# A fused attention and feed-forward block: four weight transfers by group, and two collections of the attention output in two pieces

## The chip, the core and the metric

The kernel runs on one core of one Trainium2 chip. The metric is the device time of one execution in microseconds (us), lower is better. The kernel before has a median of 215.92 us over three runs (215.3 to 215.97).

The core's engines run beside one another and wait for each other by semaphores: TensorE (PE, with its weight loads as PEld) multiplies matrices, VectorE (DVE), ScalarE (ACT) and GpSimd (POOL) work on tiles, and SyncE (SP) issues transfers. Sixteen DMA engines carry the transfers; SP and ACT each have a queue of them (q1 is SP's in the profile, q10 is ACT's).

## The reference

S = 2048 tokens, D = 448 columns, H = 16 heads of 28, F = 1792, an attention window of W = 256; all arrays are bfloat16.

```python
xn = _layernorm(x)
qkv = (xn @ wqkv).reshape(B, S, 3, H, Dh).transpose(2, 0, 3, 1, 4)
q, k, v = qkv[0], qkv[1], qkv[2]
scores = einsum("bhqd,bhkd->bhqk", q, k) * (Dh ** -0.5)
mask = (i - j >= 0) & (i - j < W)
p = softmax(where(mask, scores, -1e9))
o = einsum("bhqk,bhkd->bhqd", p, v)
attention = o.transpose(0, 2, 1, 3).reshape(B, S, D) @ wo
ffn = (gelu(xn @ w_gate) * (xn @ w_up)) @ w_down
return x + attention + ffn
```

## The kernel before

The tokens are cut into 16 tiles of 128 (t) and four blocks of 512 (qb, 0 to 3). The normalised input stands transposed in `xnT` (columns in four chunks of up to 128 partitions), and once more in `xsw` with the two halves of each chunk exchanged, so that two matmuls with 64 rows each can run on the two halves of the array. The feed-forward part reads both: a pair of matmuls per chunk, one from `xnT`, one from `xsw` (L459).

The 16 heads are four groups of four (g). The weights of q and k for all heads arrive in `wraw`, q in columns 0 to 447 and k in columns 448 to 895. Each group is then copied into `wqp` (q) or `wkp` (k), where a head has 32 columns instead of 28 (`pads`, L711 to L716). `proj` (L189 to L232) multiplies them with `xnT` into the PSUM tiles `pq` and `pk`, `qk_halves` (L197) adds the last 64 columns, and `qk_copies` (L244, L245) moves the results to `qT` and `kT`.

The order of the work is written out by hand; an engine, and the SP queue, run their instructions in the order in which the code names them. The order at the start is this. SP issues x tiles 0, 2 and 3, weights of v, the last rows of the weights (L92, L94), x tiles 4 to 7 (L95), and then at L97 the columns of groups two to four, once for q, once for k. ACT issues x tile 1 and group one of q and k (L89). Behind L97, SP issues the first part of the up weights `wu` (L82), `w3k` (L130), the exchange of `xsw` for block 0 (`swap`, L440), x tiles 8 to 11 (L745), the transposition of tile 4 (L176), the exchanged v weights `wvs` (L776) and three more transpositions. VectorE copies, behind `qk_copies` of group one (L762 to L769): group two of q, a tile of v, group two of k, groups three and four of q, groups three and four of k; then it normalises tile 4. TensorE meanwhile projects group two, computes scores (L657) as soon as the score buffer is free, and after the projections of group four begins with the up projection (`gen_up`, tile `ue`), whose first chunk reads `xsw`. There is one score buffer during attention, which the exponential on ScalarE (L661) empties.

Every transfer counts its landing on one of eight semaphores in turn (SP's and ACT's transfers together); an issue waits until the transfer eight places before it, which used the same semaphore, has landed.

Block by block, attention and the feed-forward part of one block are woven together with the output part (`gen_down`, L393) of the block before. The head dimension 28 leaves four of 32 rows unused, so heads 14 and 15 are spread over these rows. For the output this means: the fourth group's tile of `oN`, rows 64 to 123, is collected into a buffer `o3` in device memory (`o_collect`, L351, three transfers of 28, 16 and 12 rows of 512 columns) and delivered from there to the four spare rows of each 32 (`o_deliver`, L356, four transfers). `o_finish` then clears or copies rows of `oN` on GpSimd (L362 to L365), and TensorE reads them in the output part of the next block (L410 for blocks 0 and 1, the terms `os` for blocks 2 and 3). `hook` (L850) calls these after a step of the gate, `o_collect` from SP for blocks 1 to 3 and from ACT for block 0.

```python
        for t0, n, p0 in ((0, 7, 64), (7, 4, 96), (11, 3, 112)):
            queue.dma_start(out=o3[t0:t0 + n]..., in_=oNs[qb][p0:p0 + 4 * n, 3, :])
```

The later weights come in `ahead3`: the rest of the gate weights `wg` (groups of three and four column pairs), of `wu`, the output weights `wo` (L798, L799) and `wd`.

Of the kernel before, what the change touches and what calls it, by code (L numbers as in the profile page):

```python
# [16 lines left out]
S, D, H, Dh, F = 2048, 448, 16, 28, 1792  # L17
# [10 lines left out]
def kernel(  # L28
# [11 lines left out]
    nc = tc.nc  # L40
# [25 lines left out]
    wraw = blk.tile([P, 4, 2 * D], bf16, name="wraw", tag="hT")  # L66
# [5 lines left out]
    def rows(w, c0, n):  # L72
        return w[c0 * P:(c0 + n) * P, :].rearrange("(c p) n -> p c n", p=P)

    def load_ffn(dst, w, pairs):

        wv64 = w.rearrange("(c p) (h n) -> p c h n", p=64, h=2)
        ns = slice(pairs.start * P, pairs.stop * P)  # L80
        for hi in range(2):
            nc.sync.dma_start(out=dst[64 * hi:64 * hi + 64, :, ns], in_=wv64[:, :, hi, ns])  # L82

    wqk = rows(A_wqkv, 0, 3)[:, :, 0:2 * D]
# [8 lines left out]
    for a in range(2):  # L93
        nc.sync.dma_start(out=wv[64 * a:64 * a + 64, 3, :], in_=A_wqkv[384:448, 2 * D:3 * D])  # L94
    nc.sync.dma_start(out=x_sb[:, 4:8, :], in_=xv[:, 4:8, :])  # L95
    for c in (0, D):
        nc.sync.dma_start(out=wraw[:, 0:3, c + 4 * Dh:c + D], in_=wqk[:, :, c + 4 * Dh:c + D])  # L97
    load_ffn(wu, B_w_up, slice(0, 5))

    ident = const.tile([P, P], bf16, name="ident")  # L100
# [246 lines left out]

    def o_collect(qb, queue):

        for t0, n, p0 in ((0, 7, 64), (7, 4, 96), (11, 3, 112)):  # L350
            queue.dma_start(out=o3[t0:t0 + n].rearrange("t i n -> (t i) n"), in_=oNs[qb][p0:p0 + 4 * n, 3, :])  # L351

    def o_deliver(qb):
# [450 lines left out]
    for qb in range(NB):  # L804
# [45 lines left out]
        def hook(f):  # L850
            after(f)
            if qb in (1, 2) and f == 0:
                collect(qb + 1)
            if f == (8, 2, 2, 6)[qb]:
                o_collect(qb, nc.sync if qb else nc.scalar)
            if f == (12, 4, 4, 6)[qb]:
                o_deliver(qb)
                o_finish(qb)
            if qb == 0 and f == 6:
                nc.gpsimd.tensor_copy(out=wo[64:128, 3, :], in_=wo[0:64, 3, :])  # L860
            if qb in (1, 2) and f == 10:
                deliver(qb + 1)
            t = ({0: 8, 4: 9, 8: 10, 10: 11} if qb == 0 else {4: 12, 6: 13, 8: 14, 10: 15} if qb == 1 else {}).get(f)
            if t is not None:
                norm(t)
                dma_transp(t)
# [160 lines left out]
```

## Time and profile before

| | us |
|---|---|
| median of three runs | 215.92 |
| lowest and highest | 215.3, 215.97 |
| the profiled execution's own time | 215.69 |
| its span in the profile | 213.9 |
| TensorE busy in it | 208.2 |
| VectorE, ScalarE, GpSimd busy | 161.3, 130.4, 49.4 |

The granted TensorE clock is 1.0 throughout. The span runs from the first to the last instruction of the core; 1.8 us of the execution's time lie around it. A row of the timeline gives start, length, engine, line, operation, tile written and tiles read, how many instructions are merged in it, and in brackets the idle time before it with what ended it. A row with SPq or ACTq is the issue of a transfer, not the transfer. Matmuls overlap one another: one of 512 columns is shown with 0.38 us, but the next starts 0.216 us later.

### The profile page before, as it was taken

The page shows a single profiled execution, that of the slowest core. Times are in us where ns is not written, and L with a number is a line of the kernel's source. Part 1 is how long each engine was busy: PE and PEld are TensorE (multiplying, and loading weights), DVE is VectorE, ACT ScalarE, POOL GpSimd, SP SyncE. Part 2 cuts the span into 40 slices and gives each one's busy share as a digit, 9 for nine tenths or more (in the row PEclk, how much of TensorE's full clock was granted, in tenths as well). Part 3 has the DMA queues.
Part 4 walks back from the last instruction along what each step waited for, and adds up shares of the span by engine and source line. Part 5 has one row for each costly group of instructions (what it writes and reads, how often), then busy time and mean ns, then how long its engine had stood idle before and what let it go on. Part 6 is the DMA issues. An engine that isn't in the chain of part 4 may idle for free.

```text
span 213.9 us, 6417 instructions
## 1 busy us (share of the span) xinstructions
PE 208.2 (97%) x2718; PEld 100.6 (47%) x2722; DVE 161.3 (75%) x357; ACT 130.4 (61%) x121; POOL 49.4 (23%) x85
## 2 busy tenths in 40 slices
PE   7999999999999999999999999999999999999993
PEld 2433444444454545444445435444444444544892
DVE  7799998999767995796536998494449699569531
ACT  4699578566677986423777896532678577456000
POOL 5286758451000211041000202022000021106001
PEclk9999999999999999999999999999999999999999
DMA  6999989979420101003521000101000000000011
GB/s 177 274 223 213 106 199 236 216 220 181 110 56 26 36 0 41 9 5 65 74 74 46 25 0 27 22 0 35 12 26 3 21 3 25 21 3 2 26 44 50
DMA packets 23993, 15.67 MB, mean 73 GB/s; under 512 B 9208, under 2 KB 23832, under 8 KB 23960
## 3 DMA queue, kind: packets, MB, share of 16 engines
q1 hardware_dynamic: 22918, 14.87, 31.7%
q8 instruction: 22, 0.36, 0.7%
q10 hardware_dynamic: 1042, 0.34, 0.7%
q14 instruction: 11, 0.09, 0.1%
HBM read 9.26 MB, written 2.41 MB: 55 GB/s over the span
## 4 chain that ended last, share of the span: by engine, by line
PE 92%; DMA 5%; issue 1%; ACTq 0%; DVE 0%; DVEq 0%
PE po L393 26%; PE gt L459 20%; PE u L459 12%; PE ue L459 8%; PE pq L334 7%; PE sc L657 6%; DMA wraw<-in_A_wqkv_dram 5%; PE ov L627 5%; PE pv L320 4%; PE pq L191 2%; PE pk L191 1%; PE pv L191 0%; PE pq L254 0%; PE po L410 0%; PE pv L197 0%
## 5 line engine op out<-in xcount | busy, mean ns | idle before, releaser
L661 ACT ACTIVATE p_sb<-sc 128x2048 bf16<-128x2048 f32 x39 | 73.2, 1878 | 19.7 <-PE sc L657 12.1
L594 POOL TENSOR_TENSOR oN<-oc,l 128x512 bf16<-128x512 f32 x16 | 22.4, 1409 | 121.8 <-DVE l L607 121.8
L499 ACT ACTIVATE p_sb<-gt 128x1024 bf16<-128x1024 f32 x28 | 28.7, 1025 | 33.6 <-PE gt L459 30.7
L393 PE MATMUL po<-wd,hT 128*128 128x448 bf16 (+1 forms) x266 | 46.4, 324 | 0.0
L459 PE MATMUL gt<-xnT,wg 64*128 64x512 bf16 x224 | 45.6, 376 | 0.0
L459 PE MATMUL gt<-xsw,wg 64*128 64x512 bf16 x168 | 40.7, 376 | 0.0
L575 DVE TENSOR_TENSOR p_sb<-p_sb,masks 128x256 bf16<-128x256 bf16 (+1 forms) x90 | 30.3, 391 | 8.9 <-ACT p_sb L661 8.9
L507 DVE TENSOR_TENSOR hT<-p_sb,u 128x512 bf16<-128x512 bf16 x34 | 21.9, 677 | 16.0 <-PE u L459 15.8
L393 PEld LDWEIGHTS <-hT 128*128 128x128 bf16 x266 | 24.6, 98 | 16.2 <-issue 1.2
L459 PEld LDWEIGHTS <-wg 64*128 64x128 bf16 x392 | 18.6, 94 | 23.0 <-issue 1.3
L459 PEld LDWEIGHTS <-wu 64*128 64x128 bf16 x392 | 18.4, 94 | 23.1 <-issue 2.2
L459 PE MATMUL u<-xnT,wu 64*128 64x512 bf16 x136 | 28.1, 376 | 0.0
L459 PE MATMUL u<-xsw,wu 64*128 64x512 bf16 x102 | 24.7, 376 | 0.0
L382 DVE TENSOR_TENSOR res<-po,x_sb 128x448 bf16<-128x448 f32 (+1 forms) x17 | 9.9, 591 | 12.4 <-PE po L393 10.3
L459 PE MATMUL ue<-xnT,wu 64*128 64x512 bf16 x88 | 18.3, 377 | 0.0
L459 PE MATMUL ue<-xsw,wu 64*128 64x512 bf16 x66 | 16.5, 377 | 0.0
L657 PE MATMUL sc<-qT,kT 28*64 28x320 bf16 (+7 forms) x648 | 16.4, 261 | 0.0
L585 POOL TENSOR_SCALAR_AFFINE_SELECT p_sb<-p_sb 128x512 bf16<-128x512 bf16 (+1 forms) x21 | 14.2, 703 | 6.7 <-ACT p_sb L661 6.7
L657 PEld LDWEIGHTS <-kT 28*64 28x64 bf16 (+1 forms) x648 | 7.7, 102 | 13.4 <-issue 12.2
L393 PE MATMUL po<-wo,oN 128*128 128x448 bf16 (+1 forms) x72 | 13.7, 321 | 0.0
L476 DVE CAST hT<-ue 128x512 bf16<-128x512 f32 x20 | 12.8, 680 | 0.8 <-PE ue L459 0.6
L612 DVE TENSOR_TENSOR oc<-oc,ov 128x512 f32<-128x512 f32 x12 | 8.2, 686 | 5.0 <-ACT oc L611 4.9
(108 smaller groups left out, 274.4 us busy)
## 6 DMA issues: line engine op xcount, KB each, us to landing
out_dram<-res SPq DMA_DIRECT2D x15, 112.0 KB
x_sb<-in_A_x_dram SPq DMA_DIRECT2D x3, 448.0 KB
wd<-in_B_w_down_dram SPq DMA_DIRECT2D x3, 448.0 KB
xsw<-xnT SPq DMA_DIRECT2D x6, 192.0 KB
wu<-in_B_w_up_dram SPq DMA_DIRECT2D x2, 560.0 KB
wg<-in_B_w_gate_dram SPq DMA_DIRECT2D x2, 448.0 KB
wg<-in_B_w_gate_dram SPq DMA_DIRECT2D x2, 336.0 KB
wraw<-in_A_wqkv_dram SPq DMA_DIRECT2D x2, 252.0 KB
```

Of the source, the lines that this page charges most:

```text
L334: nc.tensor.matmul(ps, lhsT=w.rearrange("p h d -> p (h d)"), rhs=xchunk(qb, hi, c, qb * QB, QB), start=c == 0, stop=c == 6, tile_position= ...
L393: nc.tensor.matmul(po[:, a:b], lhsT=x[:, k, tt * P:(tt + 1) * P], rhs=wt[:, k, lo + a:lo + b], start=start and n == a == 0, stop=stop and ...
L459: nc.tensor.matmul(ps, lhsT=w[64 * hi:64 * hi + 64, c, p * P:(p + 1) * P], rhs=xchunk(qb, hi, c, qb * QB, QB), start=c == 0, stop=c == 6, ...
L476: copy(out=hTs[qb][:, p + 7 * i, :], in_=us[i])
L499: nc.scalar.activation(out=ges[p][:, :, :], in_=gt[:, :, :], func=ACT.Gelu_apprx_tanh)
L507: nc.vector.tensor_tensor(out=hT[:, p + 7 * i, :], in0=ge[:, i, :], in1=u, op=ALU.mult)
L575: nc.vector.tensor_tensor(out=reg, in0=reg, in1=m, op=ALU.mult)
L585: nc.gpsimd.affine_select(out=reg, in_=reg, pattern=mid + [[1 if diag else -1, min(w, P)]], compare_op=ALU.is_ge, fill=0.0, base=0 if diag ...
L594: nc.gpsimd.tensor_tensor(out=oN[:, g, :], in0=oc[:, :], in1=inv, op=ALU.mult)
L627: nc.tensor.matmul(ov[half or 0][32 * j:32 * j + 32, q0:q0 + nq], lhsT=v_sb[r, kt, 4 * g + j, :], rhs=p_sb[r, j, col:col + nq], start=n == ...
L657: nc.tensor.matmul(ss[k0:k0 + nk, j, col:col + nq], lhsT=kT[r, g, kt * P + k0:kt * P + k0 + nk], rhs=qT[r, g, ring(qb).start + q0:ring(qb) ...
L661: nc.scalar.activation(out=p_sb[:, :, 0:ncol], in_=ss[:, :, 0:ncol], func=ACT.Exp, scale=SCALE)
```

## The change

Two edits. The columns of groups two to four of `wraw`, which came in one transfer of 336 columns for q and one of 336 for k, come in four: group two of q (112 columns), group two of k, groups three and four of q (224 columns), groups three and four of k. `o_collect` issues, for blocks 1 and 2, two transfers of 28 rows each instead of three of 28, 16 and 12; the rows are the same, since the second and third piece lie next to each other on both sides. Blocks 0 and 3 keep three.

```diff
-    for c in (0, D):
-        nc.sync.dma_start(out=wraw[:, 0:3, c + 4 * Dh:c + D], in_=wqk[:, :, c + 4 * Dh:c + D])
+    for lo, up in ((4 * Dh, 8 * Dh), (8 * Dh, D)):
+        for c in (0, D):
+            nc.sync.dma_start(out=wraw[:, 0:3, c + lo:c + up], in_=wqk[:, :, c + lo:c + up])
...
-        for t0, n, p0 in ((0, 7, 64), (7, 4, 96), (11, 3, 112)):
+        for t0, n, p0 in ((0, 7, 64), (7, 7, 96)) if qb in (1, 2) else ((0, 7, 64), (7, 4, 96), (11, 3, 112)):
             queue.dma_start(out=o3[t0:t0 + n].rearrange("t i n -> (t i) n"), in_=oNs[qb][p0:p0 + 4 * n, 3, :])
```

With this, VectorE's copies wait for four different landings: group two of q for the first transfer, group two of k for the second, groups three and four for the third and the fourth. The lines behind the edit are numbered one higher in the changed kernel.

## The prediction

> **What bounds the kernel now.** I read the page's first part, then the chain of waits, then the stretch that the chain names, in the timeline. The chain rows are start, length, what.
>
> ```profile
> span 213.9 us, 6417 instructions
> PE 208.2 (97%) x2718; PEld 100.6 (47%) x2722; DVE 161.3 (75%) x357; ACT 130.4 (61%) x121; POOL 49.4 (23%) x85
> 7.12 5.54 DMA wraw<-in_A_wqkv_dram
> 12.68 0.29 DVE wkp L716
> 13.02 0.82 PE pk L191 x3
> ```
>
> TensorE is busy for 208.2 of 213.9 us. The chain is TensorE from 13.02 on; before that it hangs on one transfer, the k weights of groups two to four (the second one of L97), which are issued at 7.12 and landed at 12.66. A table by stretch says how much later waiting there is (columns: stretch and length, then busy us of PE, PEld, DVE, ACT and POOL, granted clock, DMA share, GB/s).
>
> ```profile
> 8.00:9.00 1.00, 1.00 (x10) 0.49 (x8) 0.55 (x3) 0.85 (x2) 0.00 (x0) 1.00 1.07 339
> 14.00:19.00 5.00, 5.00 (x39) 1.76 (x37) 4.79 (x12) 4.53 (x7) 3.77 (x7) 1.00 1.38 235
> 16.00:18.40 2.40, 2.40 (x19) 0.83 (x18) 2.26 (x6) 2.07 (x5) 1.79 (x4) 1.00 1.12 254
> 23.30:28.00 4.70, 4.70 (x54) 1.92 (x52) 4.56 (x11) 3.19 (x3) 2.63 (x8) 1.00 0.65 143
> 32.00:43.00 11.00, 11.00 (x140) 4.96 (x134) 9.74 (x19) 7.85 (x8) 7.02 (x10) 1.00 1.04 224
> 104.00:154.00 50.00, 49.95 (x725) 23.64 (x724) 33.51 (x73) 31.62 (x27) 5.84 (x5) 1.00 0.13 29
> ```
>
> From 14 us on TensorE has next to no idle time. So nothing behind that point can be gained by a wait that goes away, and whatever TensorE loses near the start it carries to the end. At the same time the DMA engines are full (share 1.0 and more) from 8 to 18.4 us and from 32 to 43 us, so a transfer made slower there pushes all that stand behind it.
>
> **The weights, part one: the wait that goes away.** These are timeline rows, with the idle time before them in brackets.
>
> ```profile
> 11.55 0.27 DVE L716 COPY wqp<-wraw 128x336 bf16<-128x336 bf16 x1
> 11.73 0.61 DVE L227 CAST v_sb<-pv 128x448 bf16<-128x448 f32 x1
> 12.02 0.82 PE L191 MATMUL pq<-xnT,wqp 128*128 128x512 bf16 x2
> 12.19 1.88 ACT L661 ACTIVATE p_sb<-sc 128x2048 bf16<-128x2048 f32 x1 [0.27 <-PE sc L657]
> 12.68 0.28 DVE L716 COPY wkp<-wraw 128x336 bf16<-128x336 bf16 x1 [0.35 <-DMA wraw<-in_A_wqkv_dram]
> 12.88 0.45 DVE L716 COPY wqp<-wraw 128x672 bf16<-128x672 bf16 x1
> 13.25 0.37 DVE L716 COPY wkp<-wraw 128x672 bf16<-128x672 bf16 x1
> 14.28 0.40 PE L657 MATMUL sc<-qT,kT 28*128 28x384 bf16 x8
> 17.81 1.88 ACT L661 ACTIVATE p_sb<-sc 128x2048 bf16<-128x2048 f32 x1
> 19.79 0.40 PE L657 MATMUL sc<-qT,kT 28*128 28x128 bf16 x8
> ```
>
> VectorE stood idle 0.35 us before it could copy group two of k. With the change this copy waits for the second of four transfers, whose last byte is number 168 KB of the stream. The q transfer of before, with 252 KB, had landed by 11.55, since its copy ran then. So the new piece lands by about 11.6 at the latest, the copy runs at 12.33, right behind the cast that starts at 11.73, and pk can follow pq without the gap: pq is three matmuls from 12.02 at about 0.216 us each (the three of pk take 0.82 with a tail of 0.39), so pk could start at 12.67 instead of 13.02. That is 0.35 us for TensorE, if nothing else holds it.
>
> Something does. The next scores (14.28) write the one score buffer, which the exponential of 12.19 leaves at 14.07. Elsewhere scores start 0.10 behind such a release (17.81 + 1.88 = 19.69, scores at 19.79), so here not before 14.17. The gain that arrives behind the scores is 0.11; the bounds are 0.11 and 0.35, and I take 0.11.
>
> The wait itself moves to the last of the four transfers, for groups three and four of k. Its copy ran at 13.25; if this piece lands when L97's second did plus what the smaller packets cost (0.5, below), that is 13.16, and VectorE gets there at 12.33 + 0.28 + 0.45 = 13.06. Nothing is lost until it lands behind 13.25; from there each tenth delays the normalisation behind it, at 13.54.
>
> **The weights, part two: two more issues.** SP's rows around the edit:
>
> ```profile
> 10.32 1.33 SPq L440 DMA_DIRECT2D xsw<-xnT  x2
> 11.70 0.61 SPq L745 DMA_DIRECT2D x_sb<-in_A_x_dram  x1
> 14.16 1.33 SPq L176 DMA_TRANSPOSE xnT<-xn  x1
> L97 SPq DMA_DIRECT2D wraw<-in_A_wqkv_dram x2: 368/438/507, 5.4 to 7.1; - x2
> ```
>
> An issue of L97 takes 0.44 us (the median in the last row), so wu, w3k, xsw and x_sb tiles 8 to 11 are issued about 0.9 us later. An issue also waits until the transfer eight places ahead has landed; with two more, every transfer from wu on is still paired with its eighth forerunner, and the new pairs of wu, w3k and xsw look back to transfers that are long in. The late issues cost nothing by themselves: the engines are full then, wu follows the weights in the queue, and xsw, issued at 11.2 instead of 10.32, has its turn after wu, at 17 us. The transposition at 14.16 waits for VectorE; x_sb would be issued by 13.2, so a microsecond of cover is left. Without this cover the price would be up to 0.9.
>
> **The weights, part three: smaller packets.** The two old transfers have 128 x 3 rows of 672 bytes each, 768 in all. The four new ones have 768 rows of 224 and 768 of 448 bytes: the same bytes, 768 more packets.
>
> ```profile
> q1 hardware_dynamic: 22918, 14.87, 31.7%
> q10 hardware_dynamic: 1042, 0.34, 0.7%
> x_sb<-in_A_x_dram ACTq DMA_DIRECT2D x1, 112.0 KB
> ```
>
> The ACT queue (q10) already carries 768 rows of 224 bytes, the group-one weights. Its share is 0.007 x 16 x 213.9 = 24.0 engine-us. In the stretch 8 to 9, where rows of 672 and 896 bytes pass, a byte costs 16 x 1.07 / 339 = 0.0505 ns, so the 112 KB of x_sb and some 56 KB of o take 8.7; 15.3 are left, or 19.9 ns a row, less a little for the 90 other packets: about 19. A row of 672 takes 33.9. A line through both puts a fixed 11 to 12 ns on each packet, and 768 / 16 x 11.5 = 0.55 us on each engine. The rounding of 0.7% moves it between 0.3 and 0.8. I take 0.5.
>
> The page "DMA: Bandwidth & Descriptors" of the Trainium skill (section Specifications) says that rows need 512 bytes for line rate and that shorter ones are read, modified and written back, which would speak against this edit more strongly than my line does: both new sizes lie below, the old one above. By that rule taken as double work the sum would be 217.1 (second rival); the ACT queue's 19 ns against 11.3 (224 x 0.0505) go some way with it, and no row here shows 448 bytes.
>
> Who is behind these packets? Everything in the queue up to xsw, whose landing TensorE needs:
>
> ```profile
> 18.82 0.39 PE L197 MATMUL pq<-xnT,w3p 64*128 64x512 bf16 x1
> 19.05 0.59 PE L459 MATMUL ue<-xsw,wu 64*128 64x512 bf16 x2
> SPq L776 <- DMA wu<-in_B_w_up_dram: 1.0, 1, 1.0
> L776 SPq DMA_DIRECT2D wvs<-in_A_wqkv_dram x2: 619/626/634, 15.5 to 17.2; - x2
> ```
>
> The second issue of wvs, at 17.2, waited for the second half of wu: so wu landed at 17.2. Then come w3k (28 KB) and xsw (2 x 192 KB), 422 KB (in bytes), at 254 GB/s 1.66 us: an estimated landing at 18.86, against 19.05 for the first matmul that reads xsw. The slack is 0.2 us. With 0.5 us more in the queue xsw lands at 19.36, and this matmul starts at about 19.37: TensorE loses 0.3 us against before, and the 0.11 won above vanishes in that wait. A full 0.8 in the queue would make it 0.6; 0.3 would make it 0.1.
>
> A second such place lies at the late gate weights:
>
> ```profile
> 43.06 0.25 SPq L799 DMA_DIRECT2D wo<-in_A_wo_dram  x1
> 43.34 0.59 PE L459 MATMUL gt<-xsw,wg 64*128 64x512 bf16 x2
> ```
>
> The issue at 43.06 waits for the second half of wg (eight places ahead), which so landed at 43.05; the first matmuls of gate pair 3 that read it are at 43.34. If the half microsecond is still in the queue by then, wg lands at 43.55, but TensorE comes 0.3 later too, at 43.64. It may as well have been made up between 23.3 and 28, where the share is 0.65. I count nothing here; without TensorE's own delay it would be 0.2.
>
> **The collections.** In blocks one and two of the queries, two issues instead of three:
>
> ```profile
> 95.06 1.15 SPq L351 DMA_DIRECT2D o<-oN  x3
> 99.08 0.29 POOL L363 COPY oN<-oN 64x128 bf16<-64x128 bf16 x1 [1.38 <-DMA oN<-o]
> 111.80 0.29 PE po L410 x2
> 147.61 0.52 POOL L365 MEMSET oN<- 64x512 bf16 x1 [2.36 <-DMA o<-oN]
> 156.89 0.34 PE sc L657 x16
> ```
>
> SP saves 1.15 / 3 = 0.38 us each time (block two's issues run the same way), and what is issued behind it (oN, transpositions, kT) may come that much earlier. Nobody waits for it: GpSimd is done with oN at 99.4 and TensorE reads those rows at 111.80; in block two GpSimd is done at 148.1 and TensorE comes to the output terms, behind the first ten of wd, close to 156. If the one piece of 28 rows should land later than the 16 and the 12, 8 us cover it. Zero, between a loss of 0 and a gain of 0.
>
> **Sum.** 0.3 us on the profiled execution's 215.69 (span 213.9, 1.8 around it): 215.99. That execution lies 0.23 below the median 215.92 of the runs, so on the median: 216.2.
>
> **Rivals.**
> 1. The queue doesn't feel the packets. From 14 us on the engines move 235 to 254 GB/s with a full share, against 339 at 8 to 9, so something else than packets limits wu; 0.5 us at its head might be made up. Against it: full engines, in order. Then xsw lands near 18.9, and TensorE keeps 0.11 to 0.35: 215.6 to 215.8.
> 2. Slower: short rows cost double. The point is xsw's landing: each tenth behind 19.05 is a tenth lost. 168 KB at 1.7 times the long rows' 0.0505 ns a byte (the ACT queue's 19 ns) and 336 KB at 2 times add 0.7 x 0.51 + 1.0 x 1.01 = 1.4 us; xsw lands at 20.2, TensorE loses 1.2: 217.1. For it speaks the ACT queue, against it that its rows only bear 1.7 for the smallest size. This is the skill's rule above as a mechanism here.
> 3. The change doesn't do what it says: the late landing at 12.66 belongs to that moment, not to the bytes, so k's group two comes late as well, or VectorE's wait just moves to the last piece, and xsw still arrives in time: 215.9.
>
> **How the numbers follow.** Forecast 45%, rival 1 27%, rival 2 20%, rival 3 8%. The forecast's own range, with 0.3 to 0.8 in the queue, is 216.0 to 216.5. I call a change within 0.3% (0.65 us) the same, about what a measurement of this kernel can tell from none. Four fifths of the forecast, most of rival 1 and all of rival 3 lie within it: 62%. Rival 2, nearly whole, and a fifth of the forecast are slower: 28%. Faster by 0.65 us isn't in any price above, as TensorE can win 0.35 at most; I leave 10% for what this one profile doesn't show. The range goes from rival 1 with its full 0.35 and the runs' own spread (215.3) to rival 2 (217.1).
>
> **What would show it.** Right: VectorE's copy of group two of k at 12.3 without a wait; pk right behind pq near 12.7; scores near 14.2; a gap of TensorE before the first matmul that reads xsw, which starts at 19.3 to 19.5; the second issue of wvs at about 17.7; from there all of TensorE shifted by the same amount to the end. Wrong: no gap before that matmul (rival 1), wvs behind 18.3 (rival 2), or a gap somewhere behind 44 us, which I have nothing for.

## The result, and the profile after

| | before | after |
|---|---|---|
| median of the runs beside each other (7 each) | 215.34 us | 216.40 us |
| lowest and highest | 215.2, 215.97 | 215.57, 217.03 |
| the profiled execution's own time | 215.69 us | 215.91 us |
| its span | 213.9 us | 214.2 us |

The ratio after to before is 1.0034 [1.0018, 1.005]: a loss of 0.34%, some 0.7 us, just beyond the 0.3% that the prediction named as the border of what can be told. (The medians lie 1.1 us apart, but the runs of each kernel scatter over 0.8 and 1.5 us; I go by the ratio with its interval.) A second measurement of the same kernel (e6) gave 1.0044 [1.0023, 1.0064]. The change makes this kernel a little slower.

From the page of the changed kernel (first part and queues: busy us and share; packets, MB, share of 16 engines):

```profile
span 214.2 us, 6414 instructions
...
PE 208.6 (97%) x2718; PEld 100.9 (47%) x2722; DVE 161.5 (75%) x357; ACT 130.4 (61%) x121; POOL 49.5 (23%) x85
...
q1 hardware_dynamic: 23690, 14.87, 30.3%
q10 hardware_dynamic: 1042, 0.34, 0.9%
```

SP's queue carries the same bytes in 772 more packets, 768 of them the weights' as counted. The place to look at is the stretch from 5 to 20 us of the timeline of the changed kernel:

```profile
5.44 3.06 SPq L98 DMA_DIRECT2D wraw<-in_A_wqkv_dram  x4
...
8.54 1.33 SPq L82 DMA_DIRECT2D wu<-in_B_w_up_dram  x2
...
11.33 1.33 SPq L441 DMA_DIRECT2D xsw<-xnT  x2
...
12.34 0.27 DVE L717 COPY wkp<-wraw 128x336 bf16<-128x336 bf16 x1
...
12.76 0.81 PE L192 MATMUL pk<-xnT,wkp 128*128 128x512 bf16 x3
...
14.20 0.40 PE L658 MATMUL sc<-qT,kT 28*128 28x384 bf16 x8
...
18.97 0.38 PE L460 MATMUL ue<-xnT,wu 64*128 64x512 bf16 x1
...
19.61 0.39 PE L460 MATMUL ue<-xsw,wu 64*128 64x512 bf16 x2 [0.27 <-DMA xsw<-xnT]
```

Group two of k is copied at 12.34 without a wait, where it waited until 12.68 before. pk starts at 12.76 instead of 13.02, the scores at 14.20 instead of 14.28. So 0.26 us won has become 0.08 behind the score buffer, and at 18.97 the first matmul of the up projection is 0.07 ahead of before (19.04). Then TensorE stands still: its partner, the first matmul that reads `xsw`, started 0.01 later before (19.05), and now comes at 19.61. The chain of waits of the changed kernel (start, length, what) hangs on this transfer, where that of before hung on the k weights:

```profile
12.02 7.45 DMA xsw<-xnT
...
196.95 13.88 PE po L394 x126
```

The same last group of the chain, 126 matmuls of the output part, started at 196.39 before:

```profile
196.39 13.87 PE po L393 x126
```

I call the place where TensorE needs `xsw` the gate, and the distance between the two matmuls the gap. The loss at the gate is 19.61 - 19.05 = 0.56 us, and at the end it is 196.95 - 196.39 = 0.56 us. Nothing between them gave or took anything. The span grew by 0.3 us alone, since the part behind the last result (210.68 before, 211.24 after) was about 0.2 us shorter in this one execution. That part returns in the experiments; I call it the close.

By stretch (length, busy us of PE, PEld, DVE, ACT, POOL, clock, DMA share, GB/s), first the changed kernel, then two stretches of before that the prediction doesn't show:

```profile
8.00:9.00 1.00, 1.00 (x11) 0.54 (x10) 0.55 (x3) 0.85 (x3) 0.00 (x0) 1.00 0.88 191
10.00:11.00 1.00, 1.00 (x7) 0.21 (x5) 0.74 (x3) 0.51 (x3) 0.90 (x5) 1.00 0.87 129
16.00:18.40 2.40, 2.40 (x19) 0.81 (x18) 2.06 (x5) 2.26 (x5) 2.00 (x4) 1.00 1.14 231
18.50:19.80 1.30, 1.03 (x7) 0.25 (x7) 1.30 (x6) 1.30 (x2) 0.25 (x1) 1.00 1.61 263
```

```profile
10.00:11.00 1.00, 1.00 (x8) 0.18 (x6) 0.93 (x5) 0.60 (x3) 0.90 (x5) 1.00 0.91 252
18.50:19.80 1.30, 1.30 (x14) 0.36 (x14) 1.30 (x7) 1.30 (x2) 0.04 (x1) 1.00 1.40 89
```

From 8 to 9 us the queue moved 191 GB/s where it moved 339, from 10 to 11 us 129 where it moved 252. In the last stretch, where before 89 GB/s moved, 263 pass now: the queue is behind, and TensorE is busy for 1.03 of 1.30 us.

### The profile page after: what moved, and what is told of

It is laid out like the page before. It is cut to its first block, busy times and chain, and to the rows that moved or that the text cites. A ratio compares the mean times of both kernels' runs of the same rounds, so it can differ in the third digit from the quotient of the medians.

```text
span 214.2 us, 6414 instructions
## 1 busy us (share of the span) xinstructions
PE 208.6 (97%) x2718; PEld 100.9 (47%) x2722; DVE 161.5 (75%) x357; ACT 130.4 (61%) x121; POOL 49.5 (23%) x85
## 4 chain that ended last, share of the span: by engine, by line
PE 91%; DMA 5%; DVE 1%; issue 1%; ACT 1%; SPq 0%; DVEq 0%
PE po L394 26%; PE gt L460 20%; PE u L460 12%; PE ue L460 8%; PE pq L335 7%; PE sc L658 6%; PE ov L628 5%; PE pv L321 4%; DMA xsw<-xnT 3%; DMA x_sb<-in_A_x_dram 1%; PE pq L192 1%; DVE st L156 1%; PE pv L192 1%; PE s L192 1%; PE pq L255 0%
```

## The experiments

Each was timed against the kernel before in alternating runs on one chip (12 runs of each experiment, 35 of before; medians of before 215.54 for e1 to e4, 215.67 for e5 to e8, 215.61 for e9 to e12). A profile shows one of the 12 runs. Where an expectation of e5 to e7 gives the closing stretch, it counts from the start of the last result, 0.4 us more than the close here.

**e7, the kernel before against itself.** No edit.

> The kernel before as its own experiment: a second profile and the size of a null result. Ratio 0.999 to 1.001; VectorE's wait for group two of k is between 0 and 0.4 us, as it was 0.35 in the first profile of before and 0 in the profile of the two-piece collections; xsw's first matmul at 18.9 to 19.1, closing stretch 3.3 to 3.6 us.

Median 215.66, ratio 1.0 [0.9983, 1.0016]. A loss of 0.3% can thus be told from none. The profile gave a second thing, the row of the copy on which the prediction's first step rests:

```profile
12.36 0.31 DVE L716 COPY wkp<-wraw 128x336 bf16<-128x336 bf16 x1
```

It doesn't wait here. The 0.35 us wait in the first profile of before belongs to that execution, not to the kernel. The traces count a landing in sixteen steps: in the first profile fifteen of the sixteen for this transfer were in by 10.58, and the last came at 12.66; here it was in at 11.88. And before itself has a small gap here, with the first up matmul at 18.99 and its partner at 19.03:

```profile
19.03 0.54 PE L459 MATMUL ue<-xsw,wu 64*128 64x512 bf16 x2
```

**e6, the change again.** No edit to the changed kernel.

> The changed kernel once more, for a second profile and more times on this chip. If its loss is the late xsw: a gap of 0.3 to 0.9 us before the first matmul that reads xsw, closing stretch 3.3 to 3.6 us, ratio 1.002 to 1.005. If the gap was an accident of one profile, the matmul at 19.05 and the loss elsewhere.

Median 216.28, ratio 1.0044 [1.0023, 1.0064]. Timeline rows, then the first of the stretches:

```profile
18.84 0.38 PE L460 MATMUL ue<-xnT,wu 64*128 64x512 bf16 x1
19.26 0.39 PE L460 MATMUL ue<-xsw,wu 64*128 64x512 bf16 x2
```

```profile
8.00:9.00 1.00, 1.00 (x10) 0.49 (x8) 0.54 (x3) 0.89 (x2) 0.00 (x0) 1.00 1.05 219
```

The gap is there again, 0.42 instead of 0.64. This execution issued `wu` at 7.79, only 0.26 later than before, and its engines were full from 8 to 9 us (1.05), but they moved 219 GB/s instead of 339.

**e1, the weights alone.** The first edit of the change without the collections.

```diff
-    for c in (0, D):
-        nc.sync.dma_start(out=wraw[:, 0:3, c + 4 * Dh:c + D], in_=wqk[:, :, c + 4 * Dh:c + D])
+    for lo, up in ((4 * Dh, 8 * Dh), (8 * Dh, D)):
+        for c in (0, D):
+            nc.sync.dma_start(out=wraw[:, 0:3, c + lo:c + up], in_=wqk[:, :, c + lo:c + up])
```

> The four weight transfers alone, collections in three pieces as before. Theory A (the smaller rows fill the queue ahead of xsw) and theory B (up weights issued 1 us later leave the queue dry) both expect all of the change's loss here: ratio 1.003 to 1.005 to before, and the first matmul that reads xsw 0.4 to 1.2 us later than in before (19.05). Theory C (the two-piece collections cost the time, through SP's order or the landing of oN) expects 1.000 to 1.001 here, although TensorE would still show the gap near 19 us.

Median 216.28, ratio 1.002 [1.0003, 1.0036]. The timeline of e1 at the gate, and its SP waits behind the last branch (line, releaser: total, times, longest):

```profile
19.03 0.38 PE L460 MATMUL ue<-xnT,wu 64*128 64x512 bf16 x1
19.87 0.39 PE L460 MATMUL ue<-xsw,wu 64*128 64x512 bf16 x2 [0.46 <-DMA xsw<-xnT]
```

```profile
SPq L902 <- SPq L902: 1.1, 2, 0.9
```

The gap belongs to the weights. The long wait behind the branch is new: in before this wait behind the branch was at most 0.5, and its close 3.2; here the last result ends at 211.51 and the span at 215.4, so the close is 3.9.

**e2, the collections alone.** The second edit of the change without the weights.

```diff
-        for t0, n, p0 in ((0, 7, 64), (7, 4, 96), (11, 3, 112)):
+        for t0, n, p0 in ((0, 7, 64), (7, 7, 96)) if qb in (1, 2) else ((0, 7, 64), (7, 4, 96), (11, 3, 112)):
```

> The two-piece collections alone, weights in two transfers as before. Theories A and B: 1.000 (0.999 to 1.001), TensorE at 19.0 to 19.1 us for the first xsw matmul as before, and no gap around 104 or 156 us. Theory C: 1.003 or more.

Median 215.68, ratio 1.0007 [0.9992, 1.0022]: nothing. No gap at the gate (both matmuls at 18.91), and group two of k again copied without a wait, from before's weights:

```profile
12.28 0.27 DVE L716 COPY wkp<-wraw 128x336 bf16<-128x336 bf16 x1
```

**e3, four transfers with the old rows.** The same number of issues and the same bytes as in the change, but cut by chunk of rows, so that each row keeps its 672 bytes and no packet is added. The collections stay as in before.

```diff
-    for c in (0, D):
-        nc.sync.dma_start(out=wraw[:, 0:3, c + 4 * Dh:c + D], in_=wqk[:, :, c + 4 * Dh:c + D])
+    for lo, up in ((0, 2), (2, 3)):
+        for c in (0, D):
+            nc.sync.dma_start(out=wraw[:, lo:up, c + 4 * Dh:c + D], in_=wqk[:, lo:up, c + 4 * Dh:c + D])
```

> Four transfers as in the change, but split by row chunk (two chunks, then one) instead of by group, so the 768 rows stay 672 bytes long: the two extra issues without the extra packets. Theory A: xsw lands as before, first xsw matmul at 19.0 to 19.1, ratio 1.000, VectorE still waits 0.35 us for group two of k. Theory B: wu is issued at about 8.5 instead of 7.5, the DMA engines show a stretch under a 0.8 share between 9.5 and 11 us, the matmul comes 0.3 to 0.6 later, ratio 1.0015 to 1.003.

Median 216.57, ratio 1.0035 [1.0014, 1.0056]. Slower, but not at the gate. Its timeline, two stretches, and SP's wait behind the branch:

```profile
18.89 0.38 PE L460 MATMUL ue<-xnT,wu 64*128 64x512 bf16 x1
18.90 0.59 PE L460 MATMUL ue<-xsw,wu 64*128 64x512 bf16 x2
```

```profile
9.00:10.00 1.00, 1.00 (x7) 0.44 (x6) 0.97 (x6) 0.11 (x1) 0.59 (x3) 1.00 0.66 181
10.00:11.00 1.00, 1.00 (x7) 0.18 (x6) 0.72 (x3) 0.59 (x3) 0.90 (x5) 1.00 0.69 135
```

```profile
SPq L902 <- SPq L902: 1.1, 2, 0.9
```

Without the short rows `xsw` was in time, though `wu` and `xsw` were issued when the change issues them (8.55 and 11.33, against 8.54 and 11.33). The last result ended at 210.54, 0.15 before that of the kernel before, and yet the span is 214.2: a close of 3.7. The stretches show what the late issues do to the queue: with `wu` at 8.55 the engines ran at two thirds for 2 us. In this execution that did not make `xsw` late.

**e4, short rows alone.** Before, with one more transfer behind `wu`: 768 rows of 32 bytes into a tile that nothing reads.

```diff
     load_ffn(wu, B_w_up, slice(0, 5))
+    filler = const.tile([P, 6, 16], bf16, name="filler")
+    nc.sync.dma_start(out=filler[:, :, :], in_=B_w_down[0:6 * P, 0:16].rearrange("(c p) n -> p c n", p=P))
```

> Before, with one extra transfer of 768 rows of 32 bytes into a tile that nobody reads, issued behind wu: extra packets in the queue ahead of xsw, and wu issued in time. Theory A: 768 x 8 to 12 ns / 16 = 0.4 to 0.6 us more queue, first xsw matmul at 19.4 to 19.6, ratio 1.0015 to 1.003. Theory B: matmul at 19.05 to 19.2, ratio 1.000.

Median 216.77, ratio 1.0048 [1.0031, 1.0065]. Page, timeline and SP's wait of e4:

```profile
q1 hardware_dynamic: 23702, 14.90, 31.0%
```

```profile
18.77 0.38 PE L461 MATMUL ue<-xnT,wu 64*128 64x512 bf16 x1
18.77 0.59 PE L461 MATMUL ue<-xsw,wu 64*128 64x512 bf16 x2
```

```profile
SPq L903 <- SPq L903: 1.1, 1, 1.1
```

784 packets more than before, and `xsw` isn't late. The 0.4 us that theory A expects at the least are less than the scatter of `xsw` among the kernels with before's weights (0.6, below), so this doesn't disprove a price for each packet. What the profile shows of the loss is again in the close: last result at 210.41, span 214.3, so 3.9.

**e5, two issues where nothing hangs on them.** Before, with two loads of 128 rows of 32 bytes, issued by SP near 150 us into a tile that nothing reads. It was made to see whether the close is a matter of SP's instructions.

```diff
+            if qb == 2 and f == 12:
+                filler = const.tile([P, 2, 16], bf16, name="filler")
+                for i in range(2):
+                    nc.sync.dma_start(out=filler[:, i, :], in_=B_w_down[i * P:(i + 1) * P, 0:16])
```

> Before, with two small extra transfers (128 rows of 32 bytes each) issued by SP in block 2 near 150 us, where nobody waits for SP: no change near 19 us, a longer SP program. In the runs so far the closing stretch, from the last VectorE result to the end of the span, was 3.3 to 3.6 us in before, the change and the two-piece collections, and 4.1 to 4.3 in the three kernels whose SP program is longer than that of before. Theory D (a longer SP program lengthens the close) expects 4.1 to 4.3 here and ratio 1.002 to 1.004. Theories A and B (only what happens up to 19 us counts) expect 3.3 to 3.6 and 1.000.

Median 216.22, ratio 1.0025 [1.001, 1.004]. SP's wait behind the branch in before and in e5:

```profile
SPq L901 <- SPq L901: 0.7, 2, 0.5
```

```profile
SPq L905 <- SPq L905: 1.9, 2, 1.7
```

The last result ends at 210.59, as in before (210.68); the span is 214.8. Two issues with nothing behind them cost 0.25%, and the profile has the whole loss after the work is done.

**e10, the same two issues, and the collections in two pieces.** e5 with e2's edit, so that SP issues as many transfers as in before.

> The late extra issues of before, with the two-piece collections, which take two issues out of SP's program again. Theory D (length of SP's program) expects the close back at 3.0 to 3.6 us, the wait behind SP's branch at 0.5 instead of 1.7, and ratio 0.999 to 1.001. If the extra transfers themselves lengthen the close, it stays at 4.1 and 1.0025.

Median 215.58, ratio 0.9998 [0.9984, 1.0012]. The loss is gone, and so is the long wait of SP:

```profile
SPq L905 <- SPq L905: 0.7, 2, 0.5
```

**e9, four transfers with the old rows, and the collections in two pieces.** e3 with e2's edit: this is the change with rows of 672 bytes.

> The changed kernel with one difference: its four weight transfers are cut by row chunk instead of by group, so their 768 rows stay 672 bytes long. Issues, their times and the length of SP's program are those of the change. If the short rows delay xsw (theory A in the form: rows of 224 and 448 bytes are slow), there is no gap before the first matmul that reads xsw, the close is 3.0 to 3.3 us and the ratio 0.999 to 1.001. If the two early issues do it (theory B), gap and ratio are the change's: 0.4 us or more, 1.003.

Median 216.1, ratio 1.0026 [1.0007, 1.0045]. The close is short again (SP waits 0.5 at most, 3.3 in all), but now the gate shows:

```profile
19.00 0.38 PE L460 MATMUL ue<-xnT,wu 64*128 64x512 bf16 x1
19.19 0.41 PE L460 MATMUL ue<-xsw,wu 64*128 64x512 bf16 x2
```

A gap of 0.19 with the same weight transfers that left none in e3's profile, though `wu` is issued earlier here (8.16) than there (8.55). Before has `xsw` at the edge as well (0.04 in e7), and an execution falls on one side or the other. The ratio asks for 0.56 us, more than this gap; this profile doesn't show the rest.

**e8, three transfers.** q in one piece, k in two (group two, then the rest), with the collections in two pieces: 384 more packets and one more issue for the weights.

```diff
+    for lo, up in ((4 * Dh, D), (D + 4 * Dh, D + 8 * Dh), (D + 8 * Dh, 2 * D)):
+        nc.sync.dma_start(out=wraw[:, 0:3, lo:up], in_=wqk[:, :, lo:up])
```

> Three weight transfers (all of q in one, group two of k, groups three and four of k) with the two-piece collections: one more early issue and 384 more packets, an SP program one issue shorter than before. Theories A and B: half of the change's delay, xsw's first matmul at 19.05 to 19.4, ratio 1.000 to 1.002. A version that beats both would need group two of k early without the late xsw: 0.999.

Median 215.89, ratio 1.0019 [1.0002, 1.0037]. The gap is 0.25, between none and the change's; the ratio's interval overlaps that of the change, so whether the price is half is not shown:

```profile
19.06 0.38 PE L459 MATMUL ue<-xnT,wu 64*128 64x512 bf16 x1
19.31 0.39 PE L459 MATMUL ue<-xsw,wu 64*128 64x512 bf16 x2
```

**e11 and e12, bytes taken out of the way.** Both load the fifth column pair of `wu` only behind x tiles 8 to 11, so 224 KB less stand ahead of `xsw`; both have the collections in two pieces in blocks 1 to 3. e11 has the weights of the change, e12 those of before.

```diff
-    load_ffn(wu, B_w_up, slice(0, 5))
+    load_ffn(wu, B_w_up, slice(0, 4))
...
     nc.sync.dma_start(out=x_sb[:, 8:12, :], in_=xv[:, 8:12, :])
+    load_ffn(wu, B_w_up, slice(4, 5))
```

> The changed kernel with the fifth column pair of the up weights (224 KB) loaded behind xsw instead of ahead of it, and two-piece collections in block 3 too, so that SP's program grows by one issue only. If xsw's landing is what TensorE waits for, it lands about 1 us earlier (18.1 to 18.7), the gap is gone, TensorE is 0.5 us earlier than in the change to the end, and the ratio to before is 0.998 to 1.000. If the gap is from something else, it stays.

> Before with the same later fifth pair and two-piece collections in blocks 1 to 3, weights in two transfers. Xsw about 1 us earlier than in before, where TensorE didn't wait for it: ratio 0.999 to 1.001. What the change's earlier group two of k is worth once xsw is out of the way is the difference to the kernel run with it: 0 to 0.35 us.

e11: median 216.09, ratio 1.0028 [1.0007, 1.0048]. e12: median 215.53, ratio 0.9995 [0.9983, 1.0008]. The first statistics and the gate, in e11 and then in e12:

```profile
3.23 0.63 DVE L156 BATCH_NORM_STATS2 st<-x_sb 128x6 f32<-128x448 bf16 x1 [0.16 <-DMA x_sb<-in_A_x_dram]
...
18.79 0.38 PE L460 MATMUL ue<-xnT,wu 64*128 64x512 bf16 x1
18.79 0.59 PE L460 MATMUL ue<-xsw,wu 64*128 64x512 bf16 x2
```

```profile
3.38 0.63 DVE L155 BATCH_NORM_STATS2 st<-x_sb 128x6 f32<-128x448 bf16 x1 [0.31 <-DMA x_sb<-in_A_x_dram]
...
18.94 0.38 PE L459 MATMUL ue<-xnT,wu 64*128 64x512 bf16 x1
18.94 0.59 PE L459 MATMUL ue<-xsw,wu 64*128 64x512 bf16 x2
```

With fewer bytes ahead of `xsw` the gap is gone, though the four short-row transfers are there, as it should be if the gap is a wait for `xsw`. The bytes are not the only difference: e11 also issued `xsw` at 10.33, where the change did at 11.33 and e6, with its gap of 0.42, at 10.75. What remains of e11's lead over e12 at 18.8 us, 0.15, it has from the first statistics on, which wait for the first x tile: from there to the first up matmul it is 15.56 us in both. So group two of k arriving earlier is worth nothing by then. e11 is nevertheless slower. SP has one issue more than in before and waits 1.1 behind the branch; but the close of 3.5 is no longer than that of e7, so where e11 loses its 0.28% is not shown, and no run has its weights without the additional issue. This version beats neither kernel, and e12 can't be told from before.

**All of them together.** "Issues" counts SP's transfers against before; "gap" is the distance from the first up matmul to its partner that reads `xsw`; "branch" is SP's longest wait behind the last branch; "close" is the span less the end of the last result.

| kernel | issues | gap | branch | close | ratio |
|---|---|---|---|---|---|
| e7 | 0 | 0.04 | 0.5 | 3.5 | 1.0 |
| e2 | -2 | 0 | 0.5 | 3.1 | 1.0007 |
| e10 | 0 | 0 | 0.5 | 3.0 | 0.9998 |
| e12 | -1 | 0 | 0.5 | 3.1 | 0.9995 |
| the change | 0 | 0.64 | 0.5 | 3.0 | 1.0034 |
| e6 (the change) | 0 | 0.42 | 0.5 | 3.1 | 1.0044 |
| e9 | 0 | 0.19 | 0.5 | 3.3 | 1.0026 |
| e8 | -1 | 0.25 | 0.5 | 3.3 | 1.0019 |
| e3 | +2 | 0 | 0.9 | 3.7 | 1.0035 |
| e4 | +1 | 0 | 1.1 | 3.9 | 1.0048 |
| e5 | +2 | 0 | 1.7 | 4.2 | 1.0025 |
| e11 | +1 | 0 | 1.1 | 3.5 | 1.0028 |
| e1 | +2 | 0.84 | 0.9 | 3.9 | 1.002 |

Every kernel without a gap beyond before's 0.04 and without more issues takes before's time; each with the one or the other is slower. The change has the gap alone. The sizes do not follow the profiles, though: six of the nine profiles of slower kernels fell on executions 0.25 to 0.8 us faster than their kernel's median, and e6's (215.74) took hardly more than the median of before. So what the profiles show is a part of the loss, and where the rest arises is open. e1 has both and should lose most; its profiled execution did (217.16, the slowest of its 12), its median did not. I leave that open.

## Why the prediction came out as it did

**The wait that goes away: right in its form, worth nothing.** Copy at 12.34 without a wait (12.33 forecast), pk at 12.76 (12.67), scores at 14.20 (14.17): 0.08 us survives the score buffer, 0.11 was taken. The step leaned on a wait of one execution, though. From the first statistics to the first up matmul the profile of before takes 19.04 - 3.32 = 15.72 us, the changed kernel 15.57, and e2 and e12 with before's weights 15.56 as well. So rival 3 was right in this much, that the late landing belonged to the moment; as a forecast of the time it fell, because `xsw` didn't arrive in time.

**Two more issues that "cost nothing by themselves": a weak reason.** Its numbers held: `wu` is issued 1.01 us later (0.9 forecast), `xsw` at 11.33 (11.2). Its reason did not. "The engines are full then" was read from before's stretches, and those are full because the issues come when they do. With the issues late the queue thins out: 129 GB/s from 10 to 11 us in the changed kernel, shares of 0.66 and 0.69 in e3 without any short row. Whether this has a price at the gate is not shown: e9 has a gap of 0.19, e3, with later issues, none.

**Smaller packets: the right place, the term about right, the slack wrong.** The first reader of `xsw` was forecast at 19.37, with 19.3 to 19.5 as the sign, and came at 19.61, in e6 at 19.26, in e1 at 19.87. By the landing counts in the traces `xsw` was complete at 18.91 in before, close to the estimate of 18.86, and at 19.48 in the change (19.12 in e6, 19.73 in e1). So the queue term was 0.57 us in this profile, 0.2 to 0.8 over the three; 0.5 was taken, out of 0.3 to 0.8. What the prediction had wrong is the slack. It let the reader start 0.01 behind the landing (19.36 and 19.37), but it starts 0.13 to 0.14 behind it in every kernel with a gap, and in before as well: 18.91 and 19.05. The slack of 0.2 was thus none, and with none the sum would have been 0.5 instead of 0.3.

One sign failed. The second issue of `wvs`, which waits for `wu`, was expected at about 17.7 and came at 17.3 (17.2 before):

```profile
L777 SPq DMA_DIRECT2D wvs<-in_A_wqkv_dram x2: 619/626/634, 15.1 to 17.3; - x2
```

In before fifteen of the sixteen counts for `wu` were in by 16.21 and the last at 17.20; in the change they were in by 17.07 and 17.29. One late count in before hid that the other fifteen came 0.9 us later in the change.

Rows or issues? `xsw` was complete between 18.29 and 18.91 in the five profiles with before's transfers ahead of it (before, e2, e5, e7, e10), at 18.48 and 19.06 with four transfers of long rows (e3, e9), and at 19.12, 19.48 and 19.73 with short ones (e6, the change, e1). e3 and the change issue at the same times, so the 1.0 us between them belongs to the rows, apart from scatter (0.6 among before's five). In these profiles, then, the rows bear most of the delay at the gate, and the late issues alone stay within before's scatter or little above it. The times don't separate them: e9 has 1.0026, the change 1.0034 and 1.0044, and the intervals overlap.

The fixed price per packet stands, somewhat smaller. At the start, in SP's queue, the median packet takes 9 ns with 32 bytes (e4, near 15 us), 16 with 224 and 25 with 448 (the change), 33 with 672 and 41 with 896 (before). A line through these has some 8 ns for each packet, where 11 to 12 were taken; by this estimate 768 packets over 16 engines are 0.4 us.

The page "DMA: Bandwidth & Descriptors" of the Trainium skill (section Specifications) has rows under 512 bytes read, modified and written back. Rows of 224 and 448 bytes did slow the queue (219 GB/s at a share of 1.05 in e6, 339 at 1.07 in before), in that direction the trace agrees; but the packet times above show no step between 448 and 672 bytes, and the doubled time that rival 2 made of it, `xsw` at 20.2 and 217.1 us, did not come.

**The second gate: right.** The issue that waits for the second half of `wg` is where it was (43.06 before):

```profile
43.07 0.25 SPq L800 DMA_DIRECT2D wo<-in_A_wo_dram  x1
```

TensorE comes 0.56 later, and has more slack there than before. The queue had made up its delay by then.

**The collections at zero: right alone, wrong in company.** e2 bears out the zero. But "nobody waits for it" overlooked SP's own end: with two more issues and without the collections' saving, SP waits 0.9 to 1.7 behind its branch (e1, e3, e5). In the change the two edits cancel there. That this saves time is shown for e5 and e10; for the weights it is not, since e1, without the collections, has a ratio of 1.002 [1.0003, 1.0036], no worse than the change.

**The sum and the rivals.** +0.3 us was forecast; the profiled execution shows +0.2 (0.56 lost at the gate, 0.2 to 0.3 less in the close, which is 3.2 in one execution of before and 3.5 in another), the ratio of the runs says +0.7 (0.34% of 215.34), more than twice the forecast. So 216.2 against 216.4 is luck in part: the median of before over the seven runs is 0.6 below that of the three on which the forecast was built. The mechanism, a shift that arises at `xsw` and stays to the end, is shown in the profiles by the chain of waits, by the same 0.56 us at the gate and at the end, and by the reader's fixed distance behind the landing. How much of the 0.7 it makes in the other executions is not shown. Rival 1 (the queue doesn't feel it) fell by the gap, rival 2 by its size.

## What to carry to other kernels

A split of an early transfer in a full queue is paid by the first consumer whose transfer stands behind it: find that consumer, and its slack, before counting what the split wins at the front. To the landing add the time until the consumer starts: 0.13 us made the difference between a slack of 0.2 and none. A wait seen in one profile may belong to that execution, so look at it in a second one before it becomes a gain in a sum. Count the issues of a queue to the end of its program: two transfers that nothing waited for cost 0.25% here, and taking away two others gave it back.

## What the runs showed of the hardware

**The end of the program goes with how many transfers SP issued.** With one or two more than before, SP's wait behind the last branch grew from 0.5 to between 0.9 and 1.7 us in five kernels out of five, and stayed at 0.5 in all nine profiles with as many or fewer. This branch steps over a general path that isn't taken. The close as a whole separates the two less clearly: 3.5 to 4.2 us against 3.0 to 3.5. At this end the instruction queue still fetches two packets in before (packets, MB, share, of the stretch from 212 us on):

```profile
q14 instruction: 2, 0.02, 1.7%
```

The page "Runtime: NRT & Kernel Launch" of the Trainium skill (section Instruction fetch mechanics) says that a taken branch to a target outside the instructions already held forces a fetch before the engine goes on, and that fetches come in fixed blocks. A program longer by a few instructions could so fall on the wrong side of a block. The trace shows fetches at this place but has them in the short closes too, so this cause is argued, not shown.

**A packet has a fixed price, and no step at 512 bytes shows.** Median packets of 32, 224, 448, 672 and 896 bytes took 9, 16, 25, 33 and 41 ns. Cutting 768 rows of 672 bytes into 1536 of 224 and 448 put the landing behind them at 19.12 to 19.73 us, where before's transfers had it at 18.29 to 18.91.

**The last of sixteen counts decides.** A landing can hang on one count: 12.66 us against 10.58 for the other fifteen in before, and it was this one that made VectorE wait.

**The start of an execution scatters.** The first statistics, which wait for an x tile, began between 3.19 and 3.44 us in the 14 profiles, and ten of them reached the first up matmul 15.56 or 15.57 us later. A tenth of a microsecond between two profiles at the gate is thus no effect of an edit before the start has been subtracted.
